# A recurrent-memory attention chain with its instructions in a fixed order, 40-key attention and all chain transfers on SyncE

## Chip, cores, metric

One core of a Trainium2 chip. The metric is device time of one launch in microseconds (us), median of several runs. The granted clock is the share of its full speed at which TensorE was clocked. In the profile, TensorE is PE (its weight loads PEld), VectorE is DVE, ScalarE is ACT, GpSimd is POOL, SyncE is SP.

## The reference, cut to what matters

Four layers, A B A B, each added to the residual after a layernorm. Layer A is a recurrence over 64 segments of 32 rows. Eight memory rows go from each segment to the next, so the segments form one chain; each has 40 rows, 32 heads of 192 and weights of 640 x 6144 for Q, K and V.

```python
mem = mem0
for s in range(n_seg):                        # 64, one after the other
    h = concat([mem, x[:, 32*s:32*s+32]])     # 8 + 32 rows, 640 wide
    q, k, v = h @ Wq, h @ Wk, h @ Wv          # 32 heads of 192
    p = softmax(mask(q @ k.T * scale))        # 40 x 40 a head
    o = (p @ v) @ Wo
    mem = o[:, :8]                            # goes into the next segment
    outs.append(o[:, 8:])
```

In the kernel the chain itself projects only 32 of the 40 rows, the memory and 24 rows of x. The other eight rows of x (the "extra" rows, called memory rows in some of the texts) do not depend on the chain; they are projected for all segments beforehand, in A-pre, and staged in HBM. Their output is finished in A-post. Layer B is linear attention over the whole sequence; the change leaves it alone.

## The kernel before

A segment has four rounds r of eight heads. Weights are cut into 60 pieces of 128 x 1536 (3 matrices x 4 rounds x 5 blocks of the 640 rows). They do not all fit into SBUF; 38 stay resident and 22 are loaded again in every segment, through a ring of three buffers of two pieces.

```python
STREAM = [(m, r) for r in range(4) for m in "KQV"][1:]     # 11 pairs: all but K of round 0
...
for r in range(NR):
    for m in "KQV":
        w = pieces(sp, m, r)                 # issues the ring load on SyncE
        ps = pqp.tile([P, 512], F32, ...)    # one PSUM bank
        for b in range(KC):                  # 5 blocks x 4 column groups of 32 rows
            for g in range(4):
                nc.tensor.matmul(ps[32*g:32*g+32, 0:384], lhsT=hT[:, b, :], rhs=rhs, ...)
        if m == "V":                         # two copies, 192 columns each
            nc.scalar.activation(out=Vp[...], in_=ps[:, 0:192], func=ACT.Copy)
            nc.vector.tensor_copy(out=Vp[:, 320:512], in_=ps[:, 192:384])
            continue
        ...                                  # ACT copy to raw, DVE 32x32 transpositions to QT or KT
    # scores: 4 mask matmuls, 16 with 32 keys of the segment, 16 with the extra keys of all 4 rounds
    # Exp (112 columns), 2 matmuls for the sums, Ln, Exp(-x), 2 multiplies
    # output: 16 matmuls with Vp and 16 with the extra V rows; 2 stores; Wo: 48 matmuls into W
...                                          # end of the segment:
wt = transpose(W); hT[:, :, 0:8] = wt[:, :, 0:8]     # the memory enters the next segment
```

The program text is in this order, but the framework orders each engine's instructions itself, so that neighbouring rounds overlap. Small transfers (rows of x, extra keys, queries and V, the stores) are issued by ScalarE. In A-pre the projections of the extra rows are copied out of a PSUM bank in four copies for K, three for Q, two for V, into padded tiles. Cuts are marked by "...".

The softmax here doesn't subtract the row's maximum and nothing guards it: scores larger than these inputs give would overflow.

## Time and profile before

| | before |
|---|---|
| time, median of 4 runs | 5,902.5 us (5,888.5 to 5,918.6) |
| two chains, 128 segments | 128 x 32.87 us = 4,207 us of the profiled 5,886 |
| TensorE without a matmul in flight, a segment | 9.3 us |
| DMA engines busy, a segment | 26.0 us |
| granted TensorE clock in the chain of layer 0 | 0.87 |

A segment is cut at the starts of the four Exp instructions of its rounds and of the transposition of W that closes it (L513). The third line is the time in which no matmul record covers the span; the fourth is the sum of the packets' times over 16 engines. The lines of the profile that carry this stand in the prediction.

One more pair, to be compared later: V's copies out of one PSUM bank in the timeline of before (start, duration, engine, line, operation).

```profile
2001.05 0.33 ACT L444 ACTIVATE Vp<-ps_qkv 128x192 bf16<-128x192 f32 x1 [0.32 <-PE ps_qkv L441]
2001.41 0.36 DVE L446 CAST Vp<-ps_qkv 128x192 bf16<-128x192 f32 x1
```

They run one after the other, on two engines: 0.72 us. Both read the same PSUM tile (a tile is what one `pool.tile` call returns; `ps_qkv` fills one bank).

### The profile page before, as it was taken

To read this page: it belongs to the slowest core of one execution; us is meant where nothing else is said; L and a number is where in the kernel's file an instruction comes from. 1 tells how busy PE (TensorE), PEld (TensorE's weight loads), DVE (VectorE), ACT (ScalarE), POOL (GpSimd) and SP (SyncE) were. 2 spreads that over 40 slices of the span, in tenths; PEclk is the share of its full clock that TensorE was granted. 3 is DMA by queue.
4 is the path that set the end of the run, shared out by engine and by line. 5 is a ranking of instruction groups with operands and counts; after the bars stand their busy time and mean duration, and the time that the engine had idled before them with its cause. 6 is when DMAs were issued, how large, how long until landed. Compare 5 with 4: busy or idle time off the path is not lost.

```text
span 5886.1 us, 223218 instructions
## 1 busy us (share of the span) xinstructions
PE 4099.0 (70%) x99706; PEld 2485.8 (42%) x99784; DVE 2193.4 (37%) x6878; ACT 1654.3 (28%) x4861; POOL 358.5 (6%) x1197
## 2 busy tenths in 40 slices
PE   3867777777777777727847677777777777777568
PEld 2634444444444444414335444444444444444343
DVE  3333333333333333227443333333333333332483
ACT  1323333333333333213112233332323332332230
POOL 0000000000000000000000000000000000000000
PEclk9988888888888888859878888888988898888789
DMA  8778777877777777540067777787877787776301
GB/s 260 189 252 286 276 281 286 284 282 276 278 280 283 269 290 279 198 132 1 21 205 192 228 282 287 288 284 274 291 276 281 285 289 278 282 284 215 114 22 33
DMA packets 547284, 1382.83 MB, mean 235 GB/s; under 512 B 209200, under 2 KB 349456, under 8 KB 546320
## 3 DMA queue, kind: packets, MB, share of 16 engines
q1 hardware_dynamic: 277520, 1216.05, 57.6%
q10 hardware_dynamic: 268800, 152.50, 9.3%
q8 instruction: 779, 12.76, 0.9%
q14 instruction: 185, 1.52, 0.1%
HBM read 1272.15 MB, written 96.25 MB: 232 GB/s over the span
## 4 chain that ended last, share of the span: by engine, by line
PE 37%; DMA 34%; DVE 12%; issue 7%; ACT 7%; ACTq 2%; SPq 1%; POOL 0%; DVEq 0%; POOLq 0%
DMA wring<-wstV 20%; PE ps_qkv L441 15%; PE ps_w L506 6%; DMA wring<-wstK 3%; DMA wring<-wstQ 3%; PE ps_pre L358 2%; ACT raw L449 2%; PE ps_num L559 2%; DMA vb<-vst 2%; PE ps_bqk L559 2%; PE ps_kv L559 2%; PE pp L536 1%; DVE QT L451 1%; ACT E L475 1%; DMA kqb<-stk 1%
## 5 line engine op out<-in xcount | busy, mean ns | idle before, releaser
L441 PEld LDWEIGHTS <-hT 128*32 128x32 bf16 x30720 | 834.4, 105 | 1007.5 <-issue 665.6
L441 PE MATMUL ps_qkv<-wring,hT 128*32 128x384 bf16 x11264 | 925.9, 351 | 317.5 <-DMA wring<-wstV 185.7
L449 ACT ACTIVATE raw<-ps_qkv 128x384 bf16<-128x384 f32 x1024 | 502.4, 491 | 1409.9 <-PE ps_qkv L441 1239.7
L506 PE MATMUL ps_w<-wo_res,OT 128*32 128x160 bf16 x24576 | 699.8, 260 | 248.3 <-ACT OT L501 80.7
L441 PE MATMUL ps_qkv<-wK,hT 128*32 128x384 bf16 x7168 | 647.5, 406 | 145.7 <-DVE hT L514 85.0
L506 PEld LDWEIGHTS <-OT 128*32 128x32 bf16 x24576 | 509.0, 106 | 532.7 <-ACT OT L501 280.5
L451 DVE STREAM_TRANSPOSE QT<-raw 128x384 bf16<-128x384 bf16 x512 | 296.2, 578 | 821.2 <-ACT raw L449 819.3
L441 PE MATMUL ps_qkv<-wQ,hT 128*32 128x384 bf16 x6144 | 566.8, 377 | 1.3 <-issue 1.2
L441 PE MATMUL ps_qkv<-wV,hT 128*32 128x384 bf16 x6144 | 460.7, 350 | 25.5 <-issue 22.0
L456 DVE STREAM_TRANSPOSE KT<-raw 128x128 bf16<-128x128 bf16 x1024 | 259.0, 291 | 510.4 <-ACT raw L449 504.8
L485 DVE TENSOR_TENSOR Pt<-E,rc 128x80 bf16<-128x80 bf16 x512 | 124.3, 243 | 766.0 <-ACT rc L483 766.0
L466 PE MATMUL ps_s<-QT,KT 128*32 128x40 bf16 x8192 | 205.9, 184 | 149.6 <-DVE QT L451 81.8
L444 ACT ACTIVATE Vp<-ps_qkv 128x192 bf16<-128x192 f32 x512 | 169.5, 331 | 463.4 <-PE ps_qkv L441 463.4
L492 PE MATMUL ps_o<-Pt,Vp 32*128 32x40 bf16 x8192 | 216.4, 181 | 93.4 <-DVE Pt L485 69.4
L492 PEld LDWEIGHTS <-Vp 32*128 32x128 bf16 x8192 | 184.7, 94 | 227.8 <-issue 204.1
L502 DVE CAST OT<-ps_o 128x240 bf16<-128x240 f32 x512 | 208.8, 408 | 145.4 <-ACT OT L501 133.3
L446 DVE CAST Vp<-ps_qkv 128x192 bf16<-128x192 f32 x512 | 180.7, 353 | 213.1 <-ACT Vp L444 202.5
L466 PEld LDWEIGHTS <-KT 128*32 128x32 bf16 x8192 | 151.0, 95 | 253.8 <-DVE QT L451 174.4
L501 ACT ACTIVATE OT<-ps_o 128x240 bf16<-128x240 f32 x512 | 190.1, 371 | 230.0 <-PE ps_o L496 215.4
L431 POOL COPY QT<-kqb 128x96 bf16<-128x96 bf16 x512 | 137.9, 269 | 1753.5 <-PE ps_s L470 1661.9
L503 POOL COPY otb<-OT 128x96 bf16<-128x96 bf16 x512 | 137.9, 269 | 1623.6 <-DVE OT L502 1623.6
L470 PE MATMUL ps_s<-QT,kb 128*32 128x16 bf16 x8192 | 197.6, 171 | 32.2 <-issue 32.0
(392 smaller groups left out, 5369.3 us busy)
## 6 DMA issues: line engine op xcount, KB each, us to landing
wring<-wstQ SPq DMA_DIRECT2D x516, 768.0 KB
wring<-wstV SPq DMA_DIRECT2D x516, 768.0 KB
wring<-wstK SPq DMA_DIRECT2D x387, 768.0 KB
kqb<-kqb ACTq DMA_DIRECT2D x128, 224.0 KB
kqb<-stk ACTq DMA_DIRECT2D x32, 512.0 KB
vb<-vst ACTq DMA_DIRECT2D x64, 256.0 KB
vb<-vb ACTq DMA_DIRECT2D x128, 128.0 KB
wo_res<-in_A_Wo_dram SPq DMA_DIRECT2D x8, 1920.0 KB
```

The source lines that it names most:

```text
L441: nc.tensor.matmul(ps[32 * g:32 * g + 32, 0:384], lhsT=hT[:, b, :], rhs=rhs, start=(b == 0), stop=(b == KC - 1), tile_position=(0, 32 * g) ...
L446: nc.vector.tensor_copy(out=Vp[:, 320:512], in_=ps[:, 192:384])
L449: nc.scalar.activation(out=raw[:], in_=ps[:, 0:384], func=ACT.Copy)
L451: nc.vector.transpose(out=QT[:, :, 8:40], in_=raw[:, :].rearrange("p (c j) -> p c j", j=32))
L456: nc.vector.transpose(out=kv[:, :, o, :], in_=rv[:, :, i, :])
L466: nc.tensor.matmul(S[32 * g:32 * g + 32, 40 * e:40 * e + 40], lhsT=KT[:, 4 * g + ks, :], rhs=QT[:, 3 * g + qc, :], start=False, stop=False ...
L470: nc.tensor.matmul(S[32 * g:32 * g + 32, 80 + 16 * e:96 + 16 * e], lhsT=kb[:, 4 * g + ks, :, :].rearrange("p r t -> p (r t)"), rhs=QT[:, 3 ...
L492: nc.tensor.matmul(O[:, g, 40 * i:40 * i + 40], lhsT=Vp[32 * g:32 * g + 32, P * blk:P * blk + P], rhs=Pt[32 * g:32 * g + 32, 40 * e:40 * e ...
L501: nc.scalar.activation(out=ov[:, 0:2, :], in_=O[:, 0:2, 0:120], func=ACT.Copy)
L502: nc.vector.tensor_copy(out=ov[:, 2:4, :], in_=O[:, 2:4, 0:120])
L506: nc.tensor.matmul(W[32 * g:32 * g + 32, 0:160], lhsT=OT[:, c, 8:40], rhs=wo[:, 12 * r + c, 160 * g:160 * g + 160], start=(r == 0 and c == 0),
L559: nc.tensor.matmul(ps[rows, n0:n0 + nn], lhsT=lhsT_fn(k), rhs=rhs_fn(k, n0, nn), **kw)
```

## The change

The intent: keep TensorE supplied by a hand-made order in which each wait is covered by other matmuls; make attention 40 keys wide, so that segment and extra keys go through the same matmuls; put every transfer of the chain on SyncE, in the order in which its waits end; stream one piece less. The diff, cut to its core:

```diff
-STREAM = [(m, r) for r in range(4) for m in "KQV"][1:]
+STREAM = {(m, r): {("K", 0): 0, ("V", 1): 1}.get((m, r), 2) for r in range(4) for m in "QKV"}
@@ A_pre
-  for i in range(3): ev.copy(out=stq[:, :, o:o + 8], in_=src[:, i])     # and four copies for K
+  ev.copy(out=st[:, :, 24*pi:24*pi+24].rearrange(...), in_=ps[:, 0:384].rearrange(...))
-  ev.copy(out=vt[:, g, 0:192], in_=ps[:, 0:192])
-  ev.copy(out=vt[:, g, 320:512], in_=ps[:, 192:384])
+  ev.copy(out=vt[:, g // 2, 384*(g % 2):384*(g % 2)+384], in_=ps[:, 0:384])
@@ A_chain
-  tile_pool(bufs=2, PSUM) as pqp
+  tile_pool(bufs=4, PSUM) as pqp, tc.manual_schedule()
-  nc.scalar.dma_start(...)      # rows, kqb, extra V, both stores
+  nc.sync.dma_start(...)
+  def v_rows(ps, g, eng):       # V of one column group: 32 rows to another partition
+      o = V[64*(g//2):64*(g//2)+32, 384*(g%2):384*(g%2)+384]
+      i = ps[32*g:32*g+32, 0:384]
+      nc.vector.tensor_copy(out=o, in_=i) if eng == "v" else nc.scalar.activation(out=o, in_=i, func=ACT.Copy)
   for r in range(NR):
+      pq = keys_or_queries(hT, "Q", r)            # 20 matmuls, then the ring load is refilled
+      if E is not None: O, OT = attend(E); extra_v(s, r)      # output of round r-1
+      to_rows(pq, "Q")
+      if E is not None: store_o(O, OT, 0, "s"); store_o(O, OT, 1, "s"); ...
+      pk = keys_or_queries(hT, "K", r); to_rows(pk, "K")
+      if E is not None: wo_round(W, r - 1, OT)
+      S = scores()                                 # 2 mask + 12 matmuls
+      E = Exp(S); extra_kq(kqb, r + 1)             # 5 small GpSimd copies
+      project(hT, pv, w, "V", first 3 blocks); sums(E); project(hT, pv, w, "V", last 2 blocks)
+      rc = Ln(S); rc = Exp(-rc)
+      v_rows(pv, 0, "v"); E = E * rc; v_rows(pv, 1, "s"); v_rows(pv, 2, "v"); v_rows(pv, 3, "s")
   # after round 3: attend, store_o on ACT and on DVE, wo_round, transposition of W
```

## The prediction

> **What bounds the kernel now.** I read the busy times by stretch first, then TensorE's waits, the DMA queues, and last one segment in the chain of waits and the timeline.
>
> Busy time by stretch (PE, PEld, DVE, ACT, POOL, then granted clock, DMA share, GB/s): the chain of layer 0; the work between the chains; the second chain; the end.
>
> ```profile
> 362.00:2375.00 2013.00, 1445.56 (x43436) 870.91 (x43432) 704.58 (x2379) 616.47 (x1769) 165.44 (x549) 0.87 0.79 281
> 2460.00:3300.00 840.00, 532.83 (x4296) 325.52 (x4335) 355.86 (x943) 177.85 (x572) 3.46 (x5) 0.82 0.39 113
> 3330.00:5360.00 2030.00, 1461.31 (x44144) 885.97 (x44144) 715.20 (x2418) 627.00 (x1798) 168.17 (x558) 0.87 0.79 283
> 5360.00:5886.00 526.00, 376.11 (x2733) 191.04 (x2772) 264.71 (x558) 114.23 (x282) 1.89 (x7) 0.86 0.23 73
> ```
>
> The chain is what matters: the transposition that closes a segment (L513) starts every 32.85 us (median over both layers), so 128 segments take 4,204 of 5,886 us; the other 1,682 us are layernorms, A-pre, A-post and B. No engine is full there, DMA is nearest at 0.79. So I asked what TensorE waits for in the 61 segments from 362.2 to 2375.1 us:
>
> ```profile
> PE ps_qkv L441 <- DMA wring<-wstV: 102.1, 92, 3.1
> PE ps_s L476 <- ACT E L475: 48.2, 61, 2.9
> PE ps_qkv L441 <- issue: 41.9, 36, 2.4
> PE ps_qkv L441 <- DVE hT L514: 41.2, 61, 0.7
> PE ps_w L506 <- ACT OT L501: 38.4, 84, 0.6
> PE ps_qkv L441 <- DMA wring<-wstQ: 27.2, 45, 2.9
> ```
>
> All of its gaps there sum to 567 us, 9.3 us a segment: 147 us for streamed weights, about 125 us with no visible cause ("issue"), the rest for ACT and DVE links. The chain of waits over one segment end shows why DMA at 0.79 still makes TensorE wait:
>
> ```profile
> 2001.04 7.45 DMA wring<-wstV
> 2012.30 0.26 DVE Pt L485
> 2013.22 0.38 ACT OT L501
> 2013.65 1.82 PE ps_w L506 x41
> 2015.49 0.36 DVE wt L513
> 2015.88 0.19 DVE hT L514
> 2016.11 1.82 PE ps_qkv L441 x18
> ```
>
> ```profile
> 2009.09 0.32 SPq L309 DMA_DIRECT2D wring<-wstK  x1
> ...
> 2019.17 0.32 SPq L309 DMA_DIRECT2D wring<-wstQ  x1
> ```
>
> After the last V block lands at 2008.5 the ring of three buffers is filled once more, and no buffer comes free until Q of the next segment is done: no weight load is issued for 10 us, and in the records of single transfers the engines are almost empty from 2013 to 2020. Between, they are full. The records give 6,144-byte packets of 271 ns on average, 0.724 of the time, so 23.8 us a segment for weights and 2.1 us for all else: 25.9 busy, 7 idle.
>
> **What the Trainium skill says.** "DMA: Bandwidth & Descriptors", section "Issuing engines are not separate DMA queues": transfers of the sync and scalar queues share the same 16 engines and interleave, a second queue only saves issue time. The trace agrees: in slices of 1 us the packets of both queues sum to 1.02 of the engines' time at most. Moving all to SyncE thus buys no bandwidth. "ScalarE: Activation LUTs", section "What ACT_TABLE_LOAD costs": an ACTIVATE with immediate scale takes 186 ns + 0.833 ns an element; the trace has 491 ns at 384 and 371 at 240, a little less. "TensorE: Matmul & The Clock Gate", section "What's actually happening": half rate after an idle window of about 3.4 us; here four column-tiled 384-wide matmuls take 0.32 us at a segment's start and 0.16 later. "Runtime: NRT & Kernel Launch", section "Instruction fetch mechanics": instructions come in 16 KiB blocks by DMA, mostly hidden. The trace has 16,384-byte packets of median 974 ns on queue 8, and unexplained TensorE gaps of up to 2.6 us while DMA is full; I suspect these fetches, not shown.
>
> **The change part by part.**
>
> *Streamed bytes.* 22 pieces of 393 KB become 21: 23.8 x 21/22 = 22.7 us a segment, plus 1.8 us for the rest (the memory rows' keys and queries shrink from 224 to 192 columns): DMA floor 24.5 us, 1.4 us less.
>
> *Attention instructions.* Per round, matmuls for mask, scores, sums and output were 4+32+2+32 = 70 and become 2+12+1+16 = 31. They are pipelined: 32 score matmuls took 0.38 us and 32 output matmuls 0.5. The new ones are wider, so I take 0.35 and 0.3: about 0.25 us a round, 1 us a segment. TensorE issues 556 instead of 712 matmuls a segment (22% less), so fewer fetches. In return V is copied in four pieces of 384 columns, two on each engine (0.49 us each on ACT; 0.57 on DVE, from 353 ns at 192 columns and 408 at 240), where two of 192 took 0.33 and 0.35; the extra keys and queries take five small GpSimd copies, about 1.1 us a round, off the path.
>
> *Fixed order.* Now TensorE does Q, output(r-1), K, Wo(r-1), scores, V. Walking a round at full clock from the start of Q: Q 0.8; V's rows end at 0.2 + 0.57 + 0.34 (multiply) + 0.57 = 1.7, so output starts at 1.8 (1.0 us idle) and takes 0.3; K ends at 2.9; the two stores of the output follow Q's eviction on ACT and end at 3.1; Wo 1.1 to 4.2 hides K's eviction (0.49) and transposition (0.58); scores to 4.55; V's resident blocks 0.48 hide Exp (0.3); sums and the last V blocks to 5.55. The best tenth of rounds before was 5.9 to 6.9 us.
>
> *Boundary.* From landing of the last V block: matmuls 0.5; V's rows 1.5; output 0.5; store 0.45; Wo 1.2 to 1.8; transposition and cast 0.65; Q 0.8 to 1.65 at half clock: 5.6 to 7.1 us until a buffer comes free, where before it was 10.7. Three loads of 2.15 us fill 6.5 of it. Engines go empty for about 1.5 us, and again for about 2 us until V of round 0 releases the second buffer. 24.5 + 3.5 = 28 us by DMA alone.
>
> *Sum of a segment.* Medians before between Exp starts of rounds 0, 1, 2, 3, then to L513, then to the next round 0: 6.84, 7.36, 8.53, 4.44, 5.66. After, estimates: 6.2 (four to five pieces to load), 6.8 and 6.9 (six pieces are 6.5 us of DMA, above the round's 5.55, plus 0.3 to 0.4 of small transfers), 4.7 (Exp 0.3, last V blocks 0.5, V's rows 1.5, output 0.5, store 0.45, Wo 1.2, handoffs; V's rows now follow the scores), 5.0 (Q before K: one eviction and transposition instead of two). Together 29.6 us: 3.25 less, 128 x 3.25 = 416 us.
>
> *A-pre.* Keys go out in one copy of 384 instead of four, queries in one instead of three, V in one instead of two. Its V part was serial: per block 1.5 us of copies, 0.5 of issue, 3.4 of DMA; I take 0.7 less for 16 blocks, 11 us, and 9 us for the key waits on the staging buffer (10.7 us each in the first round, 5.7 later): 20 us a layer, 40 us. B, A-post and layernorm stay.
>
> 5,908 - 416 - 40 = 5,452, rounded to 5,450.
>
> **The rivals.** (1) *DMA hides everything*: if the mid-segment is bound by weights alone, and the ring runs empty as before, only the one piece and little else is won: 1.4 us plus 1 us, 128 x 2.4 + 40 gives 5,560. For: DMA is full in mid-segment. Against: the weight waits are only 147 of 567 us, and the boundary gets shorter. (2) *V's rows take the place of the old waits*: 1.0 us idle a round, four times, plus the ACT order with stores behind evictions. If each round costs 0.5 us more than walked, 128 x 2 = 256 us return: 5,700. For: ACT rises from some 10 to about 14 us a segment. Against: rounds wait for DMA anyway, so part is hidden. (3) *One queue in order*: a store at the segment end that waits for GpSimd, which waits for the memory rows queued behind three loads, holds back the refill of Q behind it: 1 us a segment, 5,580. (4) *Everything overlaps*: segments at the two floors of 28 us and below, with fetch stalls gone: 5,200.
>
> **Range and chances.** Segments of 28.0 to 31.2 us span 5,245 to 5,655; that is my range 5,240 to 5,660. Within 2% (above 5,790) needs segments over 32.2 us, that is both (2) and (3) in full. Faster 0.92, same 0.06, slower 0.02.
>
> **What would show it.** Right: L513's successor every 29 to 30 us; DMA share in the chain up to 0.83 to 0.88 at unchanged GB/s while full; the issue gap at segment ends 10 down to about 7 us; "issue" gaps fewer; TensorE's largest engine wait on V's rows or the multiply before the output matmuls, about 1 us; A-pre 20 us shorter. Wrong: a SyncE wait on the output store or on memory rows ahead of the Q load with empty DMA engines; packets much slower or faster than 271 ns; rounds of 5.6 us (DMA was no floor) or above 7.5.

## The result and the profile after

| | before | after |
|---|---|---|
| time, median of 4 runs each | 5,902.5 us | 5,666.6 us (5,656.3 to 5,693.5) |
| ratio | | 0.9609, 95% interval 0.9573 to 0.9645 |
| profiled run | 5,886.1 | 5,690.9 |
| first Exp of the first chain | 334.4 | 301.9 |
| last Exp of the first chain to first Exp of the second | 865.0 | 832.0 |

Ratios are the mean time of one kernel's runs over the mean of the other's of the same rounds, so not quite the ratio of the medians. The predicted 5,450 us and its range, 5,240 to 5,660, are missed, by 7 us at the range's end; "faster by over 2%" is right. The profiled run of after is the slowest of its four, 27 us above the median, or 0.2 us a segment, so differences of traces to after's are too large by up to that.

Of the 195 us between the two profiled runs, the chain has 128 x (32.87 - 31.83) = 133 and A-pre 65 (32.5 + 33.0). The prediction had 416 and 40. So the loss is in the chain:

| a segment, us (means of both layers) | before | predicted | after |
|---|---|---|---|
| Exp of round 0 to round 1 | 7.08 | 6.2 | 6.44 |
| round 1 to 2 | 7.55 | 6.8 | 6.52 |
| round 2 to 3 | 8.34 | 6.9 | 7.21 |
| Exp of round 3 to the closing transposition | 4.37 | 4.7 | 6.22 |
| closing transposition to Exp of round 0 | 5.53 | 5.0 | 5.44 |
| sum | 32.87 | 29.6 | 31.83 |

The first chain in the busy times (PE, PEld, DVE, ACT, POOL, clock, DMA share, GB/s), with TensorE's longest waits below it:

```profile
362.00:2275.00 1913.00, 1454.54 (x33296) 865.36 (x33296) 774.41 (x2157) 845.68 (x2157) 293.42 (x1439) 0.89 0.78 275
```

```profile
PE ps_o L495 <- DVE Vp L469: 113.5, 180, 1.8
PE ps_s L484 <- DVE KT L457: 110.8, 215, 1.4
PE ps_qkv L443 <- DMA wring<-wstQ: 49.8, 62, 1.8
PE ps_qkv L443 <- DVE hT L582: 40.7, 60, 0.8
```

A segment has 22% fewer matmuls (556 for 712), yet matmul records cover no smaller a part of the stage than before (1,454 of 1,913 us, 0.76; 1,446 of 2,013 before, 0.72), and DMA is no fuller, 0.78 against 0.79: 25.1 us of a segment busy, 6.7 empty. Weight waits fell from 147 to 71 us (with K and V, not shown here). The longest wait is new: the output matmuls wait for V's copies. The second, nearly as long, is the scores' wait for K's transposition. 59% of the rounds (95% of the first, 73% of the second, 9% of the third) last 6.40 to 6.44 us, which says that a fixed chain of instructions sets them. The timeline shows which (one round):

```profile
2000.04 0.55 DVE L469 CAST Vp<-ps_qkv 32x384 bf16<-32x384 f32 x1 [1.76 <-PE ps_qkv L443]
2000.51 0.30 DVE L566 TENSOR_TENSOR E<-E,rc 128x160 bf16<-128x160 bf16 x1
2000.62 0.48 ACT L471 ACTIVATE Vp<-ps_qkv 32x384 bf16<-32x384 f32 x1 [0.36 <-DVE Vp L469]
2001.13 0.56 DVE L469 CAST Vp<-ps_qkv 32x384 bf16<-32x384 f32 x1 [0.32 <-ACT Vp L471]
2001.72 0.48 ACT L471 ACTIVATE Vp<-ps_qkv 32x384 bf16<-32x384 f32 x1 [0.62 <-DVE Vp L469]
2001.74 0.87 PE L495 MATMUL ps_o<-E,Vp 40*128 40x40 bf16 x15 [0.68 <-DVE Vp L469]
```

The four copies alternate between DVE and ACT, and the brackets say that each waits for the one before on the other engine. All ACT copies, 1,024 of 1,024, waited so (519 us in the view of this line). From 2000.04 to 2002.20 they take 2.16 us; the prediction let the engines work side by side and had 1.5. All four read one PSUM tile, which lies in one bank, and the semaphores that the framework placed run the two engines in turn. Before had that too, for two copies. Whether they go by the bank or by the tile, e1 does not tell, as it changes both; e11 tells more.

The end of the same segment, where Wo of the last round and then Q of the next run at half clock:

```profile
2022.13 0.37 ACT L508 ACTIVATE OT<-ps_o 128x240 bf16<-128x240 f32 x1 [0.61 <-PE ps_o L495]
2022.54 0.41 DVE L506 CAST OT<-ps_o 128x240 bf16<-128x240 f32 x1 [1.15 <-ACT OT L508]
2022.56 1.79 PE L513 MATMUL ps_w<-wo_res,OT 128*32 128x160 bf16 x48 [0.56 <-ACT OT L508]
2024.40 0.35 DVE L581 STREAM_TRANSPOSE wt<-ps_w 128x160 f32<-128x160 f32 x1 [1.46 <-PE ps_w L513]
2025.03 1.15 PE L443 MATMUL ps_qkv<-wQ,hT 128*32 128x384 bf16 x12 [0.68 <-DVE hT L582]
```

Elsewhere in after the same 48 Wo matmuls take 1.00 us. Between the first and the last start of the 48 there are 1.45 us when the clock is halved; this is so in 61% of the segment ends of after and in 75% of before. Exp of round 3 to the closing transposition is 6.28 us (median) in the halved ones and 5.46 in the others.

The DVE store of the output waits for ACT's there, too (1.15 us), but Wo starts as soon as ACT's half is done.

So three theories, to be told apart: the chain of V's copies sets the round; the half clock sets the segment end; or DMA (ring and bytes) is the floor whatever the engines do.

### The profile page after: what moved, and what is told of

It is laid out like the page before. It is cut to its first block, busy times and chain, and to the rows that moved or that the text cites. A ratio compares the mean times of both kernels' runs of the same rounds, so it can differ in the third digit from the quotient of the medians.

```text
span 5690.9 us, 186473 instructions
## 1 busy us (share of the span) xinstructions
PE 4165.3 (73%) x79816; PEld 2489.4 (44%) x79816; DVE 2323.7 (41%) x6110; ACT 2122.3 (37%) x5373; POOL 631.5 (11%) x3095
## 4 chain that ended last, share of the span: by engine, by line
PE 47%; DMA 23%; DVE 18%; ACT 7%; issue 3%; ACTq 1%; SPq 0%; DVEq 0%; POOL 0%; POOLq 0%
PE ps_qkv L443 20%; DMA wring<-wstK 9%; DVE Vp L469 7%; PE ps_o L495 6%; PE ps_w L513 5%; DMA wring<-wstQ 4%; DVE KT L457 3%; ACT raw L455 3%; PE ps_pre L358 3%; ACT Vp L471 3%; PE ps_s L484 2%; PE ps_num L627 2%; PE ps_bqk L627 2%; PE ps_kv L627 2%; DMA Vp<-vb 2%
## 5 line engine op out<-in xcount | busy, mean ns | idle before, releaser
L469 DVE CAST Vp<-ps_qkv 32x384 bf16<-32x384 f32 x1024 | 563.6, 550 | 1121.7 <-PE ps_qkv L443 960.1
L443 PE MATMUL ps_qkv<-wring,hT 128*32 128x384 bf16 x10752 | 749.2, 353 | 146.7 <-DMA wring<-wstQ 97.5
L495 PE MATMUL ps_o<-E,Vp 40*128 40x40 bf16 (+1 forms) x8192 | 507.7, 197 | 423.0 <-DVE Vp L469 253.2
L455 ACT ACTIVATE raw<-ps_qkv 128x384 bf16<-128x384 f32 x1024 | 501.9, 490 | 520.8 <-PE ps_qkv L443 498.9
L471 ACT ACTIVATE Vp<-ps_qkv 32x384 bf16<-32x384 f32 x1024 | 493.3, 482 | 519.4 <-DVE Vp L469 519.4
L495 PEld LDWEIGHTS <-Vp 40*128 40x128 bf16 (+1 forms) x8192 | 319.3, 100 | 749.4 <-DVE Vp L469 315.6
L443 PE MATMUL ps_qkv<-wQ,hT 128*32 128x384 bf16 x6144 | 407.1, 377 | 117.0 <-DVE hT L582 85.5
L443 PE MATMUL ps_qkv<-wK,hT 128*32 128x384 bf16 x7168 | 455.4, 377 | 0.0
L457 DVE STREAM_TRANSPOSE KT<-raw 128x384 bf16<-128x384 bf16 x512 | 295.9, 578 | 250.1 <-ACT raw L455 248.2
L484 PE MATMUL ps_s<-QT,KT 128*40 128x40 bf16 (+1 forms) x6144 | 183.9, 190 | 239.4 <-DVE KT L457 239.1
L358 PE MATMUL ps_pre<-xBT,wring 128*128 128x128 bf16 x1344 | 184.4, 221 | 4.4 <-DMA wring<-in_A_Wq_dram 3.2
```

The lines of the kernel that those rows point to most:

```text
L358: nc.tensor.matmul(ps[:, P * i:P * i + P], lhsT=w[b][:, P * c:P * c + P], rhs=xBT[:, b, :, 16 * tb:16 * tb + 16], start=(b == 0), stop=(b ...
L443: nc.tensor.matmul(ps[32 * g:32 * g + 32, 0:384], lhsT=hT[:, b, :], rhs=rhs, start=(b == 0), stop=(b == KC - 1), tile_position=(0, 32 * g) ...
L455: nc.scalar.activation(out=raw[:], in_=ps[:, 0:384], func=ACT.Copy)
L457: nc.vector.transpose(out=KT[:, :, 0:32], in_=raw[:, :].rearrange("p (c j) -> p c j", j=32))
L469: nc.vector.tensor_copy(out=o, in_=i)
L471: nc.scalar.activation(out=o, in_=i, func=ACT.Copy)
```

## The experiments

e3, e5, e6, e8 and e11 build on e1, the others on after. The kernel before ran in the rounds of each; the ratios below are to it, and after's is 0.9609. After itself was not run again, so it is compared with the others through these ratios, whose intervals are 0.2 to 0.4 points to each side.

**e1: V in two PSUM tiles, and so in two banks.**

```diff
-pv = pqp.tile([P, 512], F32, name="ps_qkv", tag="qkv")
+pv = [pqp.tile([P, 512], F32, name="ps_qkv", tag="qkv") for _ in range(2)]
-nc.tensor.matmul(ps[32*g:32*g+32, 0:384], ...)
+pg = ps[g % 2] if m == "V" else ps
+nc.tensor.matmul(pg[32*g:32*g+32, 0:384], ...)
-i = ps[32*g:32*g+32, 0:384]          # v_rows: even g on DVE, odd g on ACT, as before
+i = ps[g % 2][32*g:32*g+32, 0:384]
```

> V's projection goes to two PSUM banks, column groups 0 and 2 to one, 1 and 3 to the other, so VectorE and ScalarE no longer read one bank in turn. Theory (the four V copies wait for one another, 2.2 us in a row, and this chain sets the round): the copies overlap, the span from the first to the end of the last falls from 2.2 to about 1.4 us, rounds from 6.42 to 5.8, Exp of round 3 to the closing transposition from 6.3 to 5.6, a segment from 31.8 to 29.5, the kernel to about 5380. Rival (streaming of weights is the floor): rounds stay above 6.4 because waits for the ring take the place, the kernel stays above 5600.

Measured: 5,614 us, ratio 0.9546 (0.9520 to 0.9572), correct. The same place in its timeline:

```profile
1913.54 0.55 DVE L470 CAST Vp<-ps_qkv 32x384 bf16<-32x384 f32 x1 [1.75 <-PE ps_qkv L444]
1913.79 0.99 ACT L472 ACTIVATE Vp<-ps_qkv 32x384 bf16<-32x384 f32 x2
1914.35 0.56 DVE L470 CAST Vp<-ps_qkv 32x384 bf16<-32x384 f32 x1
```

The two ACT copies are one merged row now, beside DVE's: 1913.54 to 1914.91, 1.37 us instead of 2.16. The undisturbed round is 5.90 us, as expected 5.8. But only the first round keeps it (92% within 0.03 us; mean 5.95); the second stays at 6.52 in the mean and the third at 7.39, and the segment is 31.24. Waits for streamed weights rise from 71 to 135 us over about the same stretch. So the V chain did set the round, and much of what its removal frees is taken by the ring: I had expected 5,380.

**e2: half the streamed bytes; e3: the same with e1.**

```diff
-ns = STREAM[m, r]
+ns = min(1, STREAM[m, r])                  # load the first piece of a pair only
-... + [t[:, i, :] for i in range(ns)]
+... + [t[:, 0, :] for i in range(ns)]      # and use it twice: wrong result on purpose
```

> Every streamed pair of pieces loads only its first piece and uses it twice: wrong result on purpose, half of the streamed bytes. Theory (latency chain): rounds stay at 6.42, only the waits for the ring, some 1.2 us a segment, and the late V rows of the memory go; a segment about 30.2, the kernel about 5450. Rival (DMA floor): a segment falls by several us, the kernel under 5250.

> Both edits together, wrong result on purpose: the latency floor once the copies overlap and weights never wait. Theory: rounds 5.7 to 5.8, a segment about 28, the kernel about 5180, and the two edits together win at least their sum, since a faster chain runs into the ring. Rival (DMA floor): the win of the two equals that of half the bytes alone.

Measured: e2 5,523 us, ratio 0.9386; e3 5,246 us, ratio 0.8913. Their outputs are wrong, which doesn't matter for the times. In e2 all three rounds are 6.42 us in the mean, none waits for weights; in e3 all three are 5.90. Taken alone, the V chain is worth 0.6% of before's time and half the bytes 2.2%; together 7.0%. Neither is "the" floor: in after the round's chain (6.42 us) and six pieces with small transfers (6.5 to 6.9 us) lie so close that removing one uncovers the other (the 6.5 to 6.9 us are the prediction's estimate from 1.1 us a piece, not a measurement). The prediction's own floor of 28 us for DMA alone stands beside e3's 28.5 for the chain.

**e4: after without the fixed order.**

```diff
-tile_pool(bufs=1, PSUM) as pop, tc.manual_schedule():
+tile_pool(bufs=1, PSUM) as pop:
```

> The chain of after without the fixed order: the framework orders the instructions of each engine itself, everything else kept. Theory that the fixed order is what wins: slower than after by 3% or more, 5850 and up. Rival (the win is from A-pre and fewer attention instructions): within 1% of after's 5667.

Measured: 5,920 us, ratio 1.0059 (1.0032 to 1.0086). The segment is 33.66 us, longer than before's 32.87, though the instructions are after's. So the new attention and the single queue, in an order that is not theirs, cost 0.8 us a segment, one piece less notwithstanding; the order wins 1.83 us, 4.5% of the time, and is what makes the change a gain. The clock in this chain is 0.81, the lowest of all, and Wo of the segment end is at half clock in all 126 segments (61% in after), so part of what the order wins may be the clock's; this was not separated.

**e7: small transfers back on ScalarE.**

```diff
-nc.sync.dma_start(out=V[64*G+32:64*G+40, :], ...)     # and rows, kqb, both stores
+nc.scalar.dma_start(out=V[64*G+32:64*G+40, :], ...)
```

> After with only the small transfers (rows, keys and queries, V of the memory rows, both stores) moved back to ScalarE's queue; weights stay on SyncE. Theory (ScalarE is in the round's chain and each issue costs it 0.35 us): slower than after by 1 to 3%, about 5750. Rival (one queue makes small loads wait behind three weight loads): faster, 5600.

Measured: 6,191 us, ratio 1.0502 (1.0479 to 1.0524): 9% slower than after. The issue of the extra V rows waits for the output matmuls, and on ScalarE it now stands ahead of Q's eviction (the copy out of PSUM, L455):

```profile
1999.81 0.48 ACT L471 ACTIVATE Vp<-ps_qkv 32x384 bf16<-32x384 f32 x1 [0.62 <-DVE Vp L469]
1999.83 0.87 PE L495 MATMUL ps_o<-E,Vp 40*128 40x40 bf16 x15 [0.68 <-DVE Vp L469]
2000.74 0.66 ACTq L434 DMA_DIRECT2D Vp<-vb  x2
2001.45 0.49 ACT L455 ACTIVATE raw<-ps_qkv 128x384 bf16<-128x384 f32 x1 [1.16 <-DMA Vp<-vb]
```

The round becomes 7.26 us (median). From V's last copy to Q's eviction ScalarE now takes 1.16 us where after has 0.03 (medians of 384 rounds each): 0.46 for the output matmuls to end, 0.66 for the two issues, 0.05 until the eviction starts. So both count, the wait in the engine's own order and, more, the issue time, which my expectation named. In this order the queue belonged on an engine with nothing else to do.

**e5: e1 and matmuls that keep the clock; e10: these alone.**

```diff
+def warm(n):
+    D = pqp.tile([P, 512], F32, name="ps_warm", tag="qkv")      # never read
+    for _ in range(n):
+        nc.tensor.matmul(D[:, :], lhsT=self.ident[:, :], rhs=wo[:, 0, 0:512], start=True, stop=True, ...)
 # end of a segment
+warm(6)
 O, OT = attend(E)
+warm(2)
 ...
 wo_round(W, NR - 1, OT)
+warm(3)
```

> Two V banks as in e1, plus eleven 128x128x512 matmuls a segment into an unread PSUM bank, put where TensorE stands idle at the segment end (6 before the last output matmuls, 2 after them, 3 before Q of the next segment). Theory (TensorE falls to half clock in these gaps: in 61% of the segments of after the last Wo takes 1.45 us instead of about 0.9): the granted clock in the chain rises from 0.88 to over 0.95, Exp of round 3 to the closing transposition and on to the next Exp fall together from 11.4 to about 10 us, a segment to 29.9, the kernel to about 5450. Rival (a shorter boundary only empties the ring earlier): rounds 1 to 3 lengthen by as much, the kernel stays above 5560. If the extra matmuls are in the way instead, it is slower than e1.

> After with the eleven extra matmuls a segment of e5, but with V in one bank. Theory (the two causes are additive, the clock costs about 1.3 us a segment): ratio to before falls from 0.961 to about 0.935. Rival (the serial V copies leave the gap too long to be filled by six matmuls, so the clock still drops): 0.95 or more.

Measured: e5 5,480 us, ratio 0.9293 (0.9268 to 0.9318); e10 5,505 us, ratio 0.9339 (0.9307 to 0.9372); both correct. Wo of the segment end is at half clock in 3% and 1% of the segments, the granted clock in the chain is 0.97 and 0.98. In e5:

```profile
2005.13 1.47 PE L521 MATMUL ps_warm<-wo_res,ident 128*128 128x512 bf16 x5
2007.25 0.60 PE L521 MATMUL ps_warm<-wo_res,ident 128*128 128x512 bf16 x2
2007.88 1.04 PE L514 MATMUL ps_w<-wo_res,OT 128*32 128x160 bf16 x48
```

1.04 us for the 48 matmuls where after has 1.79. The two segment-end terms are 5.68 and 4.43 us in e10, against 6.22 and 5.44 in after: 1.55 us, and 1.4 remain in the whole segment (31.83 to 30.43); by the ratios, which after's slow trace does not touch, it is 1.2. Unlike e1's gain most of this one stays. Eleven useless matmuls a segment save 2.7% of before's time.

**e6: the next segment's extra keys and queries loaded earlier (on e1).**

```diff
+if r == 2 and s + 1 < NSEG: kqb = load_kqb(s + 1)      # after the refill of V of round 2
-    kqb = load_kqb(s + 1)                               # was: after the scores of round 3
```

> Two V banks as in e1, and the load of the next segment's keys and queries of the memory rows is issued after V of round 2 instead of after the scores of round 3, so that GpSimd and the output store behind it no longer hold SyncE at the segment end (1 us a segment in after). Theory (one queue in order holds back the refill of Q): SyncE's wait for the output copy goes, weights flow about 0.5 us earlier, kernel 40 to 90 us faster than e1. Rival (the ring, not SyncE, is what is late): within 0.5% of e1.

Measured: 5,647 us, ratio 0.9572 (0.9542 to 0.9602), against e1's 0.9546: no gain. In after, SyncE does wait at the output store as rival 3 foresaw:

```profile
SPq L577 <- POOL otb L576: 60.8, 39, 3.2
```

That is 1 us a segment (81.6 us in all in e1), and the edit leaves 15.1 us of it. But the load now stands ahead of extra V rows in the queue; TensorE's waits for these double (35 to 68 us) and the way from Exp of round 3 to the transposition grows from 5.85 to 6.33 us. The other four terms of the segment together are 0.1 us shorter than in e1, so hardly any time hung on the wait on SyncE; how much an edit would win that does not delay V's rows was not run.

**e8: K of round 3 resident instead of K of round 0 (on e1).**

```diff
-STREAM = {... {("K", 0): 0, ("V", 1): 1} ...}
+STREAM = {... {("K", 3): 0, ("V", 1): 1} ...}
```

> Two V banks as in e1, and K of round 3 instead of K of round 0 is the matrix that stays resident: the same bytes, streamed earlier in the segment. Theory (DMA is not full but idle for 6 to 7 us at the segment end and late in rounds 2 and 3): the third round falls from 7.4 to under 6.4, round 2 from 6.5 to about 6.1, a segment by about 1.2 us, kernel about 5460. Rival (bytes alone count): no change, within 0.5% of e1.

Measured: 5,729 us, ratio 0.9715 (0.9690 to 0.9740), slower than e1. The third round does fall, 7.39 to 6.73 us, but the first rises from 5.95 to 7.12, as its K must now come through the ring; the rest is about 19 us of A-pre, which starts with a streamed matrix. The empty 6 us of DMA at the segment end did not go: the wait moved. My expectation failed, and so did the rival, since the place of the bytes does count.

**e12: 22 pieces streamed, as before.**

```diff
-STREAM = {... {("K", 0): 0, ("V", 1): 1} ...}
+STREAM = {... {("K", 0): 0} ...}
```

> After with V of round 1 streaming two pieces instead of one, 22 of 60 as before. Theory (neither DMA nor chain alone is the floor): one piece is 1.1 us of DMA a segment and about half of it shows, 70 us, ratio 0.973. DMA floor: 140 us, ratio 0.985. Latency chain alone: no change, 0.961.

Measured: 5,747 us, ratio 0.9755 (0.9723 to 0.9787). The 22nd piece costs 1.46 points of 5,895 us, some 86 us, as expected between the two rivals: about 15 us of it by the start of the chains, the rest 71 / 128 = 0.55 us of a segment, half of a piece's 1.1 us. The two traces show only 0.28 us a segment, as after's is its slowest run and e12's its fastest: a quarter to a half of the piece. So the piece saved is, by the ratios, over a third of the change's gain.

**e9: A-pre's copies cut up again.**

```diff
-ev.copy(out=st[:, :, 24*pi:24*pi+24]..., in_=ps[:, 0:384]...)
+for i in range(3): ev.copy(out=st[:, :, o:o + 8], in_=ps[:, P*i:P*i+P]...)
-ev.copy(out=vt[...384], in_=ps[:, 0:384])
+for i in range(2): ev.copy(out=vt[...192], in_=ps[:, 192*i:192*i+192])
```

> After with the staging copies of A-pre cut up again: keys and queries in three copies a bank instead of one, V in two. Theory (the merged copies are most of the 33 us a layer by which A-pre is shorter): first Exp of the chain about 20 us later in each layer, kernel about 40 us or 0.7% slower than after, 5705. Rival (the shorter stores and the missing padding do it): under 10 us a layer.

Measured: 5,702 us, ratio 0.9675 (0.9637 to 0.9713). The first Exp comes 14 us later, the second chain's 10 us: about a third to a half of the 33 us a layer (24 us in all; by the ratios the edit costs 39). The remainder (K's fourth copy and half-partition copies, padding, smaller stores, one streamed piece less) I did not separate; e12 puts 5 and 10 us of it on the piece.

**e11: e5 with the output in two PSUM tiles.**

```diff
-O = pop.tile([P, 2, 512], F32, name="ps_o", tag="o")
+O = [pop.tile([P, 512], F32, name=f"ps_o{G}", tag=f"o{G}") for G in range(2)]
```

> e5 with the output in two separate PSUM tiles, so that at the segment end ScalarE and VectorE store its halves at the same time instead of in turn. Theory (two readers of one tile wait for each other even in different banks): 0.4 us less per segment end, 50 us, ratio to before about 0.921. Rival: the ring takes it back, 0.929 as e5.

Measured: 5,479 us, ratio 0.9295 (0.9260 to 0.9330): the same as e5. DVE's wait for ACT's store goes, as the two stores show (in e5 DVE's starts 0.40 us after ACT's, here 0.04; medians):

```profile
2009.49 0.37 ACT L509 ACTIVATE OT<-ps_o 128x240 bf16<-128x240 f32 x1 [0.94 <-PE ps_o L496]
2009.53 0.41 DVE L507 CAST OT<-ps_o 128x240 bf16<-128x240 f32 x1 [0.47 <-PE ps_o L496]
```

In one tile the halves lay in two banks and DVE still waited for ACT; in two tiles it does not. So two banks alone do not free two readers of one tile. Whether two tiles in one bank would was not run, so V's copies needed the second tile, and perhaps the second bank. But nothing is won in time. The rival named the right ratio for a wrong reason: the ring takes nothing, since there was nothing to take. Wo starts when ACT's half is done and reaches DVE's half later, so the way from the last output matmul to Wo is 0.53 us for 0.56.

e5 (or e11) is the best version found: 3.3% faster than after and 7% than before.

## Why the prediction was wrong

*Bound and place, right.* The chain was the place, and no engine its bound. The old ring gap at the segment end shrank (9.2 us between weight loads before, 7.5 after, medians; predicted 10 to 7). Packets stayed at 272 ns (271 expected). One reading was loose: the packets' sum of "1.02 at most" in slices of 1 us holds for the segment read there; over the whole first chain it is up to 1.04.

*Streamed bytes, right in size.* DMA busy a segment: 25.1 us, predicted 24.5. e12 shows a quarter to a half of a piece's time on the path.

*The round walk, the step that failed first.* The walk put V's rows at "0.2 + 0.57 + 0.34 (multiply) + 0.57 = 1.7", that is DVE alone, with ACT beside it; the overlap of the two engines did not happen. The copies in turn took 2.16 us and ended 2.39 us after the start of Q, and the undisturbed round was 6.42 us instead of 5.55. The trace of before held the hint (two copies of one tile, one after the other; DVE's store of the output waiting for ACT's), and I read these as engine times only. e1 shows the term: 1.37 us for the copies, round 5.90. The other 0.35 us are smaller errors of the walk: in the undisturbed rounds of e3 the scores start 1.47 us after Wo where the walk had 1.1, as Wo does not quite hide K's eviction and transposition (TensorE's second longest wait in after), K starts 0.12 late and V with the sums takes 0.12 more, while K and the scores take 0.25 less. The rounds' own sum came out nearly right (19.9 predicted, 20.2 measured) because the DMA allowance above 5.55 hid the mistake.

*The segment end, where the sum broke.* "4.7 (Exp 0.3, last V blocks 0.5, V's rows 1.5, output 0.5, store 0.45, Wo 1.2, handoffs)" measured 6.22: V's rows 2.16, Wo 1.79 where the clock is halved. I had seen the half clock at the segment start and gave Wo "1.2 to 1.8" in the text, then put the low end into the sum; likewise Q "0.8 to 1.65". The two segment-end terms are 1.96 us over their estimates, 250 us in all, more than the miss of 217. e10 shows 1.2 to 1.4 us a segment to be the clock.

*With both terms repaired the number holds.* e5, in which V's rows overlap and the clock stays, takes 5,480 us where I had predicted 5,450. That is some luck in the parts (its third round is 7.4 us, not 6.9).

*A-pre* was mis-sized the other way, 65 us for 40.

*The rivals.* (2), V's rows take the place of the old waits, came true in kind; that its 5,700 lies near the result is partly luck, as the half clock, which no rival named, is the larger part of the miss (1.2 to 1.4 us a segment; e1 wins 0.3 us by the ratios, 0.6 by the traces). (1) is half true: e2, e3, e12. (3) was seen and cost hardly anything: e6. (4) no.

*The check "DMA share up to 0.83 to 0.88"* told it: it stayed at 0.78, as the chain did not get short enough.

*Left open.* TensorE's gaps with no visible cause fell from about 125 us to about 3 over a chain, more than 22% fewer instructions explain; e4, in the framework's order, has only 13 too. I suspected instruction fetch, and no run shows it.

## What to carry to other kernels

Before you count two engines as working side by side on one result, look in the trace whether the second waits for the first: here one PSUM tile read in quarters by two engines was a serial chain, and two tiles in two banks cost a few lines. When two limits lie within half a microsecond of each other, as here a round's chain and its six pieces, test them together: singly they won 0.6% and 2.2%, together 7%. At the serial end of a recurrence look at the clock as well as at the waits: filler matmuls in gaps that must exist anyway may be the cheapest gain, and a DMA queue whose transfers wait belongs on an engine with nothing else to do.

## What the Trainium skill lacked or had wrong

- "TensorE: Matmul & The Clock Gate", "Why this matters for your kernels", asks for no idle gaps over about 3 us. Here that is not enough: from Exp of round 3 to the next Q of after the longest single gap between matmul records is 0.89 us (median), the gaps sum to 2.8 us of 6.9, and still 61% of the segment ends run Wo at half clock; with the gaps at 0.29 us in sum (e10) it is 1%. In the 7 us before the start of each of the 82 half-clock stretches of after's first chain, no gap between matmul records is longer than 2.4 us. The same page, under "A second HAM failure mode: psum-queue depth-cycling", does say that short idles between bursts can throttle the clock, but gives no length or share for them. Its two states, under "What's actually happening", are confirmed: the clock records hold only 0.5 and 1.0.
- "DMA: Bandwidth & Descriptors", "Issuing engines are not separate DMA queues", says a second issuing engine only saves issue time, which is usually small. What it lacks is the cost on an issuing engine that also computes: with small transfers on ScalarE instead of SyncE the kernel is 9% slower (e7), since two issues of 0.66 us in all, and 0.46 us of waiting for what they need, hold back the instructions behind them.
- "PSUM — Partial Sum Buffer", "PSUM bank collisions raise a hardware error", says that different quadrants of one bank may be accessed at once by two engines. The program did not use this: V's four copies read four different quadrants of one bank, and its semaphores ran them in turn, 2.16 us against 1.37 from two tiles in two banks (e1). As V's copies never ran at once in one bank, the page's statement itself is not tested. I found no page that says that this framework also puts two readers of one tile in turn when they read different banks (0.40 us between the output's two stores in e5, 0.04 in e11).
